# A softcap attention with a maxout layer behind it: another order of the same steps

## The chip, the cores and the metric

The kernel runs on one core of one Trainium2 chip. The metric is the device time of one execution in microseconds; three executions were timed, and a fourth was profiled. Engine names as in the profile: PE is TensorE, DVE is VectorE, ACT is ScalarE, POOL is GpSimd, SP is SyncE; PEld is TensorE's loading of weights.

## The reference

```python
batch, n_heads, seq, head_dim = (8, 12, 448, 64)
scale = 1.0 / np.sqrt(q.shape[-1])
scores = scale * np.matmul(q, k.transpose(0, 1, 3, 2))
scores = cap * np.tanh(scores / cap)
scores = scores - np.max(scores, axis=-1, keepdims=True)
attn = np.exp(scores)
attn = attn / (np.sum(attn, axis=-1, keepdims=True) + 1e-09)
attn_out = np.matmul(attn, v)
# x: 3584 tokens of 768, the heads side by side
h1 = x @ w1          # 768 x 1024
h2 = x @ w2
g = np.maximum(h1, h2)
out = g @ w_out      # 1024 x 768
```

All inputs and the output are float32 in memory; the cap is 30.

## The kernel before

**The mathematics it uses.** max(h1, h2) is h2 + relu(h1 - h2). So the kernel forms wd = w1 - w2 once (six chunks of 128 rows; `sub c e`, line 392, on DVE for e = 0 and on POOL for e = 1) and wm = w2 @ w_out once (the "premultiply": transposes of w2 `W`, copies `WC`, matmuls `P`, copies `PC`). Then out = relu(x @ wd) @ w_out + x @ wm. No maximum is subtracted before the exponential, since the tanh bounds the scores.

**Pairs and batches.** Two heads make a pair i (48 of them), two pairs make a double pair t (24), three of these a batch b. For pair i the scores are made in three key blocks j of 128 keys (`S i j`, line 502, into one of two score tiles in PSUM, s0 and s1), `T i j` is the tanh (line 507), `E i j0 j1` the exponential (line 524), both on ACT. The last 64 keys of both pairs of t are done together: `L t`, `TL t`, `EL t`. Exponentials are multiplied with v: `VL t` and `V t u j0 j1` (line 595), which also live in a score tile. `Y t` (line 561) sums the exponentials with a matmul by ones; from t = 3 on DVE has added the blocks before it (`A`, `B`, lines 536 and 541). Then DVE turns the sums to one column per 32 (`Y1`, line 566), takes the reciprocal (`Y2`, 569), turns it back (`Y3`, 572), and multiplies: `N t 0` (607, one instruction) and `N t 1` (610, two). The result is xT, the input of the dense part, in bfloat16. `N t 1` also frees the score tile that V t wrote, and `S 2t+3 2` is the next to use that tile.

**The dense part.** 120 groups g of matmuls: for each batch eight of stage 1 (relu(x @ wd), 448 columns, six units) and then three or four tiles times two halves of stage 2 (384 columns, fourteen units, 6 from x @ wm and 8 from g @ w_out). `O g bank` opens a group in one of four PSUM banks; `M x y n` (line 634) runs n steps, in each of which group x uses the upper 64 rows of TensorE and group y the lower 64 at the same time; -1 is none, x = y is one full step (line 629). A group's two halves add into one bank, one after the other: between them stands a hand-over, `Hs g` (a no-operation in SP's queue) or `H g` (in DVE's queue), which waits for the first half's last matmul and for which the second half waits. `ev g` copies a finished group out of PSUM on DVE: relu to gT (line 655, 448 columns) or to the output tile osb (line 691, 384 columns). `st b t` stores a tile from SP's queue. The dense steps fill TensorE's time between the steps of attention.

**The order.** It is written out as one string, ORDER: a list of steps. The kernel issues them one by one; each engine gets its instructions in that order, and a scheduler adds only the semaphores. So the string settles, for every engine by itself, what stands in front of what. Steps of different engines do not wait for each other unless data or a buffer make them.

**Loads.** All loads but the first k and q go through POOL's queue: `lk`, `lq`, `lv` (k, q, v of a pair or double pair), `lw1 c`, `lw2 c` (a chunk of w1 or w2), `lwo half part` (a part of w_out). They take eight semaphores in turn; a load waits until the load eight places before it has landed. From pair 10 on q and k are turned by a DMA transpose in SP's queue (`cr t`); before, by TensorE (`Xh`, `X`, copied by `XCh`, `XC`, line 453). `D bank n` are n matmuls on a constant tile, issued while TensorE has nothing else in the head.

The lines that run the string:

```python
    for s in ORDER.split(";"):
        if s.strip():
            name, *args = s.split()
            STEPS[name](*[int(a) if a.lstrip("-").isdigit() else a for a in args])
```

and those that tell which score tile a step takes:

```python
    TURN = (0, 1, 0, 1, 1, 0)
    def s_tile(turn, t):
        return s_psum.tile([P, 2, 512], f32, name=f"s{turn ^ (t % 2)}")
```

## Time and profile before

| what | value |
| --- | --- |
| three executions | 340.76, 341.51, 338.12 us; median 340.76 |
| the profiled execution | 337.93 us |
| its span, first to last instruction | 335.9 us, so 2.0 us lie around it |
| TensorE's granted clock | 0.998 |
| matmuls | 4,216 |
| bytes moved by the DMAs | 45.91 MB, mean 137 GB/s |
| largest group on ACT | L507 (tanh), 144 instructions, 925 ns each, 126.0 us |
| largest groups on PE | L634: 115.5, 101.4 and 96.4 us busy |
| L634 of wd (448 columns), one matmul | 349 ns; the two halves of a step run beside each other, and steps overlap |
| L655 copy with relu, DVE | 64 of 621 ns |
| L691 copy to osb, DVE | 54 of 555 ns |

How to read it: PE's records are pipelined, so that their durations overlap; from start to start a step of 448 columns takes 0.19 us, one of 384 columns 0.16. A wait is named with the engine that ended it ("PE s L502 <- DVE xT L610": scores on TensorE waited for DVE's writing of xT). POOL's instructions include the issuing of loads, about 0.5 to 0.9 us each.

The span has three stretches: a head up to about 57 us, in which weights are loaded and prepared and the first three double pairs are computed; a middle up to about 298 us, in which attention and dense steps are mixed; a tail of dense steps alone.

### The profile page before, as it was taken

Reading aid. Unit: us, or ns where it says so; the run is one execution under the profiler, and the core shown is the slowest. Engines: PE = TensorE matmul, PEld = TensorE weight load, DVE = VectorE, ACT = ScalarE, POOL = GpSimd, SP = SyncE. Lnnn points to the kernel's source line nnn. Section 1 sums busy time; section 2 is a strip of 40 time slices with the busy share of each in tenths; the row PEclk is TensorE's granted clock in tenths of the full one; section 3 lists DMA queues with packets and bytes.
Section 4 is the critical chain, followed back from the end, with each engine's and each line's share of the span. In section 5 each row is a group of like instructions: output and inputs, shape, how many; then the busy total and the mean of one; then the engine's idle time right before and its main releaser. Section 6 shows DMA issues by size and latency. Waiting matters only on the chain.

```text
span 335.9 us, 9947 instructions
## 1 busy us (share of the span) xinstructions
PE 322.6 (96%) x4216; PEld 196.7 (59%) x4216; DVE 244.2 (73%) x430; ACT 276.5 (82%) x267; POOL 175.4 (52%) x257
## 2 busy tenths in 40 slices
PE   8799999999999999999999999999999999999993
PEld 6654444566456555655555565675566555757972
DVE  1146879888788887987798789967988879785321
ACT  4699998999999999999999999989999999900000
POOL 7586879957645664853864687367188220000000
PEclk9999999999999999999999999999999999999999
DMA  8999999999999999989999999999999953013033
GB/s 131 203 160 229 152 251 109 158 128 89 210 172 97 102 209 213 101 110 157 141 162 109 143 191 212 101 115 166 168 130 115 202 118 79 2 47 96 2 96 94
DMA packets 136204, 45.91 MB, mean 137 GB/s; under 512 B 116448, under 2 KB 131168, under 8 KB 136160
## 3 DMA queue, kind: packets, MB, share of 16 engines
q0 software_dynamic: 96416, 25.08, 75.9%
q1 hardware_dynamic: 39440, 19.86, 27.7%
q8 instruction: 33, 0.54, 0.6%
q10 hardware_dynamic: 304, 0.33, 0.3%
q14 instruction: 11, 0.09, 0.1%
HBM read 47.45 MB, written 11.01 MB: 174 GB/s over the span
## 4 chain that ended last, share of the span: by engine, by line
PE 73%; DMA 11%; DVE 5%; ACT 4%; POOL 3%; issue 2%; POOLq 0%; DVEq 0%
PE mm L634 55%; PE s L502 7%; PE s L595 6%; DMA wo_sb<-in_moe_w_out_dram 4%; DMA gT<-in_moe_w_dram 2%; DMA kqs<-in_k_dram 2%; ACT e L524 2%; DMA xT<-in_moe_w_dram 2%; PE s L516 2%; DVE xT L610 1%; PE mm L561 1%; PE s L587 1%; ACT e L507 1%; POOL wd_sb L392 1%; PE mm L629 1%
## 5 line engine op out<-in xcount | busy, mean ns | idle before, releaser
L507 ACT ACTIVATE e<-s 128x896 bf16<-128x896 f32 x144 | 126.0, 925 | 12.7 <-PE s L502 12.5
L524 ACT ACTIVATE e<-e 128x2688 bf16<-128x2688 bf16 (+2 forms) x72 | 122.8, 1707 | 0.0
L634 PE MATMUL mm<-wo_sb,gT 64*128 64x384 bf16 x864 | 115.5, 323 | 0.0
L634 PE MATMUL mm<-wm_sb,xT 64*128 64x384 bf16 x648 | 101.4, 323 | 0.1
L634 PE MATMUL mm<-xT,wd_sb 64*128 64x448 bf16 x768 | 96.4, 349 | 0.9 <-DVE wd_sb L392 0.7
L339 POOL DMA_DIRECT2D kqs<-in_k_dram x76 | 54.4, 719 | 59.2 <-DMA qkT<-kqs 58.4
L634 PEld LDWEIGHTS <-gT 64*128 64x128 bf16 x864 | 61.8, 94 | 22.4 <-issue 1.1
L634 PEld LDWEIGHTS <-wd_sb 64*128 64x128 bf16 x768 | 50.8, 94 | 25.5 <-DVE wd_sb L392 1.1
L634 PEld LDWEIGHTS <-xT 64*128 64x128 bf16 x648 | 51.5, 94 | 16.8 <-issue 1.2
L502 PE MATMUL s<-qkT 64*128 64x448 bf16 x288 | 52.3, 355 | 2.7 <-DVE xT L610 2.3
L357 POOL DMA_DIRECT2D vp<-in_v_dram x48 | 30.5, 641 | 28.5 <-PE s L502 28.2
L655 DVE TENSOR_SCALAR gT<-mm 128x448 bf16<-128x448 f32 x64 | 39.2, 621 | 5.4 <-PE mm L634 4.0
L691 DVE COPY osb<-mm 128x384 f32<-128x384 f32 x54 | 29.1, 555 | 19.0 <-PE mm L634 18.2
L595 PE MATMUL s<-e,vp 128*32 128x448 bf16 x576 | 36.4, 354 | 0.0
L339 POOL DMA_DIRECT2D kqs<-in_q_dram x38 | 35.1, 925 | 1.7 <-DMA osb<-in_moe_w_dram 1.0
L536 DVE TENSOR_TENSOR esum<-e 128x896 bf16<-128x896 bf16 x42 | 26.4, 629 | 10.7 <-ACT e L524 10.4
L502 PEld LDWEIGHTS <-qkT 64*128 64x128 bf16 x288 | 17.8, 94 | 23.6 <-issue 15.7
L610 DVE TENSOR_TENSOR xT<-s,inv 64x448 bf16<-64x448 f32 x48 | 29.9, 622 | 0.7
L701 ACT COPY osb<-mm 128x192 f32<-128x192 f32 x1 | 0.3, 319 | 36.5 <-DMA out_dram<-osb 36.5
L536 DVE TENSOR_TENSOR esum<-esum,e 128x896 bf16<-128x896 bf16 x42 | 26.2, 623 | 5.1 <-ACT e L524 4.2
L357 POOL DMA_DIRECT2D vl<-in_v_dram x48 | 29.5, 625 | 0.0
L566 DVE STREAM_TRANSPOSE st<-mm 128x448 f32<-128x448 f32 x24 | 15.6, 650 | 15.8 <-PE mm L561 13.9
(57 smaller groups left out, 282.6 us busy)
## 6 DMA issues: line engine op xcount, KB each, us to landing
out_dram<-osb SPq DMA_DIRECT2D x54, 192.0 KB, 4.1
vp<-in_v_dram POOLq DMA_DIRECT2D x38, 160.0 KB, 4.0
kqs<-in_q_dram POOLq DMA_DIRECT2D x47, 112.0 KB, 4.8
kqs<-in_k_dram POOLq DMA_DIRECT2D x76, 56.0 KB, 3.4
wo_sb<-in_moe_w_out_dram POOLq DMA_DIRECT2D x4, 384.0 KB, 6.6
osb<-in_moe_w_dram POOLq DMA_DIRECT2D x2, 512.0 KB, 5.3
osb<-in_moe_w_dram POOLq DMA_DIRECT2D x4, 256.0 KB, 6.4
kqs<-in_k_dram POOLq DMA_DIRECT2D x9, 112.0 KB, 5.6
```

What stands on the lines that cost most here:

```text
L339: nc.gpsimd.dma_start(out=to, in_=x)
L357: nc.gpsimd.dma_start(out=to, in_=x)
L502: nc.tensor.matmul(s[:, h, :S], k_of(t, o, h, j), q_of(t, o, h))
L507: nc.scalar.activation(expo[i][:, 2 * j : 2 * j + 2, :], slots[i, j][:, :, :S], AF.Tanh, scale=scale / cap)
L524: nc.scalar.activation(e, e, AF.Exp, scale=float(cap))
L536: nc.vector.tensor_add(d, e[:, 0:2, :] if j == 1 else d, e[:, 2 * j : 2 * j + 2, :])
L566: nc.vector.transpose(st.rearrange("p b c -> p (b c)"), sums[t][:, :S])
L595: nc.tensor.matmul(vals[t][place(m, u), u, :S], w[:, m, :], expo[2 * t + o][:, 2 * j + h, :], start=False, stop=(j == NJ - 1))
L610: nc.vector.tensor_mul(x[r : r + 64], vals[t][r : r + 64, u, :S], sums[t, 3][64 - r : 128 - r])
L634: ins = nc.tensor.matmul(self.ps, w[r], x[r], start=first, stop=self.at == [self.n, self.n]).ins
L655: nc.vector.tensor_relu(gT[b // 2][:, f, cs], ps)
L691: nc.vector.tensor_copy(o[:, hs], ps)
```

## The change

ORDER is replaced by another order of almost the same steps. Counted by step: 101 matmuls `D` instead of 104; `M` steps 1,177 in both, `P` steps 96 in both; `H` 21 instead of 17 and `Hs` 107 instead of 110; the banks of many groups differ. Ten copies of stage 2 (groups 100 to 103 and 112 to 117) are now `eva`, which copies on ACT instead of DVE. `sub 4` is on DVE instead of POOL, so that only `sub 5` is left on POOL. `lwo 0 0`, the first part of w_out, is the first load in POOL's queue. A step name `lw1s` is added and not used. Nothing in the functions changes but the table of steps.

The start, the stretch with the subtractions, the turns at t = 5, 11 and 17, and the turn into the tail (the rest of the string is left out; it is changed nearly throughout):

```diff
-ld0 k; ld0 q; ms0; lk 1 0; dm; ms; D 3 3; lw2 2; D 3 5; id; D 3 5; lwo 0 0; D 3 7; lq 1 0; D 3 5; lw2 0; cd k;
...
-D 3 2; XC 1; D 3 1; E 0 0 3; D 3 10; lv 0 0; D 3 1; L 0; D 3 19; lv 0 1; W 3 2; TL 0; D 3 4; WC 3; D 3 7;
-S 1 0; lv 0 2; W 1 3; T 1 0; W 2 0; lv 0 3; WC 1; W 0 1; EL 0; lk 4 0; WC 2; S 1 1; S 1 2; T 1 1; lq 4 0; WC 0;
...
-V 1 1 2 3; Y1 1; sub 5 1; S 5 0; OP 3 1 0; P 3 1 2; Y2 1; P 3 1 2; Y3 1; P 2 1 3; T 5 0; P 2 1 1; N 1 0; O 0 2;
-M 0 -1 1; X 6 1; lw1 2; EL 2; N 1 1; lw1 1; S 5 1; T 5 1; PC 2 1; S 5 2; lq 8 0; XC 6; T 5 2; W 4 3; lw1 4;
-S 6 0; E 5 0 2; lk 8 0; WC 4; X 7 1; lk 9 0; S 6 1; XC 7; lq 9 0; OP 4 0 3; P 4 0 3; sub 2 0; T 6 0; P 4 0 1;
...
-E 6 0 3; lk 11 0; X 8 3; Y1 2; V 2 0 2 3; lk 11 1; XC 8; V 2 1 2 3; S 7 0; Y2 2; X 9 0; lv 3 0; T 7 0; Y3 2;
-lv 3 1; OP 5 1 3; P 5 1 2; XC 9; P 5 1 1; EL 3; P 5 1 1; sub 4 1; S 7 1; N 2 0; P 5 0 2; T 7 1; P 5 0 1; N 2 1;
-P 5 0 1; P 5 1 4; OP 4 1 0; P 4 1 3; PC 5 0; lv 3 2; S 7 2; S 8 0; PC 5 1; lv 3 3; T 7 2; P 4 1 2; A 3 0 1;
-P 4 1 2; lv 4 0; P 4 1 1; E 7 0 2; sub 3 0; M 0 -1 1; S 8 1; lv 4 1; M 0 -1 1; lv 4 2; PC 4 1; M 0 -1 2; T 8 0;
...
-V 5 1 2 3; Y1 5; S 13 0; M 13 12 1; lv 7 0; M 13 12 1; Y2 5; M 13 12 3; Y3 5; lv 7 1; O 14 3; M 14 12 2; Hs 13;
...
-V 11 1 2 3; Y1 11; S 25 0; lk 30 1; M 43 42 2; Y2 11; M 43 42 3; Y3 11; lv 13 0; M 43 42 3; T 25 0; st 2 1;
...
-V 23 0 2 3; V 23 1 2 3; Y1 23; M 100 101 1; ev 100; O 103 3; M 103 101 3; Y2 23; M 103 102 2; ev 101;
-M 103 102 3; Y3 23; M 103 102 4; N 23 0; M 103 102 2; O 104 1; M 104 102 2; N 23 1; Hs 103; M 104 102 1;
...
+ld0 k; ld0 q; ms0; lwo 0 0; dm; ms; D 3 5; lw2 2; D 3 5; lk 1 0; D 3 5; id; D 3 5; lq 1 0; D 3 3; cd k; D 3 1;
...
+XC 1; D 3 11; lwo 0 1; D 3 1; L 0; D 3 13; TL 0; D 3 6; lk 3 0; D 3 1; W 3 2; D 3 1; lq 4 0; D 3 1; S 1 0;
+WC 3; T 1 0; lv 0 0; W 1 3; EL 0; W 2 0; lv 0 1; WC 1; W 0 1; lv 0 2; WC 2; S 1 1; S 1 2; lv 0 3; T 1 1; WC 0;
...
+V 1 1 0 2; Y 1 0; lv 2 3; sub 0 0; E 4 0 3; V 1 0 2 3; V 1 1 2 3; Y1 1; S 5 0; O 0 1; M 0 -1 1; lq 7 0;
+P 3 0 2; Y2 1; P 2 1 1; Y3 1; lw1 2; P 2 1 2; T 5 0; X 6 0; lw1 1; N 1 0; P 2 1 1; EL 2; P 3 0 1; N 1 1; S 5 1;
+sub 5 1; P 3 0 2; T 5 1; P 3 0 1; XC 6; S 5 2; PC 2 1; T 5 2; W 4 0; PC 3 0; S 6 0; E 5 0 2; WC 4; OP 3 1 2;
+P 3 1 1; lk 8 0; X 7 3; lw1 4; S 6 1; XC 7; lq 8 0; P 3 1 2; T 6 0; P 3 1 1; sub 2 0; OP 4 0 0; P 4 0 1;
...
+P 4 0 1; E 5 2 3; L 3; PC 3 1; VL 2; V 2 0 0 2; TL 3; PC 4 0; V 2 1 0 2; lq 11 0; Y 2 3; sub 4 0; E 6 0 3;
+lk 10 0; V 2 0 2 3; X 8 2; Y1 2; lk 10 1; V 2 1 2 3; XC 8; S 7 0; lk 11 0; X 9 0; Y2 2; T 7 0; Y3 2; lk 11 1;
+M 0 -1 2; EL 3; N 2 0; OP 5 0 3; P 5 0 1; lv 3 0; S 7 1; P 5 0 1; N 2 1; P 5 0 1; T 7 1; P 5 0 1; OP 5 1 2;
...
+P 4 1 2; lv 4 2; P 4 1 1; sub 3 0; P 4 1 3; T 8 0; lv 4 3; P 4 1 1; A 3 1 1; lk 12 0; T 8 1; M 0 -1 1; S 8 2;
...
+V 5 0 0 2; V 5 1 0 2; Y 5 0; E 12 0 3; V 5 0 2 3; V 5 1 2 3; Y1 5; S 13 0; M 13 11 1; lv 7 0; M 13 11 1; Y2 5;
...
+V 11 0 2 3; V 11 1 2 3; Y1 11; S 25 0; lk 30 0; M 43 41 2; Y2 11; M 43 42 2; Y3 11; lv 13 0; M 43 42 4; N 11 0;
...
+M 100 101 4; Y 23 3; V 23 0 2 3; V 23 1 2 3; Y1 23; M 100 101 3; Y2 23; O 103 3; M 103 101 2; Y3 23; eva 100;
+M 103 101 1; M 103 102 2; eva 101; M 103 102 1; N 23 0; M 103 102 3; N 23 1; M 103 102 5; O 104 0; M 104 102 3;
...
```

Steps between Y t and S 2t+3 2 that stand on PE and DVE, counted in the whole strings:

| t | M steps before | on DVE between Y1 and N t 1, beside the chain | M steps after | on DVE after |
| --- | --- | --- | --- | --- |
| 5 | 10 | none | 18 | none |
| 11 | 15 | A 12 0 1 | 18 | none |
| 17 | 18 | ev 71, A 18 0 1 | 18 | none |
| 12 | 18 | ev 46 | 22 | ev 46, ev 47 |
| 15 | 20 | ev 60, H 62 | 18 | ev 61 |

## The prediction

> **What bounds the kernel now.** I read the page's engine shares first, then the chain that ended last, then who waited for whom, then the timeline around the longest waits.

> ```profile
> span 335.9 us, 9947 instructions
> PE 322.6 (96%) x4216; PEld 196.7 (59%) x4216; DVE 244.2 (73%) x430; ACT 276.5 (82%) x267; POOL 175.4 (52%) x257
> PE 73%; DMA 11%; DVE 5%; ACT 4%; POOL 3%; issue 2%; POOLq 0%; DVEq 0%
> PE s L502 <- DVE xT L610: 2.3, 4, 0.8
> ```

> TensorE is the bound: 96% busy, 73% of the chain. Its work cannot shrink here. Counted in both orders, the M steps number 1,177, with the same 1,131 pairs, 18 single halves and 28 full steps; at 384 or 448 columns per step they stream for 200.5 us in each. So the time can change only through TensorE's pauses: in the head, which ends at 57.28 us, in the middle, and at the turn into the tail. The last row above is the pause of the middle: scores that wait for VectorE's normalisation (N t 1) to free a score tile. The worst of them, t = 11, on VectorE, then TensorE, then ScalarE:

> ```profile
> 156.60 0.65 DVE L566 STREAM_TRANSPOSE st<-mm 128x448 f32<-128x448 f32 x1 [0.74 <-PE mm L561]
> 157.29 0.24 DVE L569 RECIPROCAL rs<-st 128x14 f32<-128x14 f32 x1
> 157.56 0.65 DVE L572 STREAM_TRANSPOSE inv<-rs 128x448 f32<-128x448 f32 x1
> 158.27 0.62 DVE L536 TENSOR_TENSOR esum<-e 128x896 bf16<-128x896 bf16 x1
> 158.82 0.62 DVE L607 TENSOR_TENSOR xT<-s,inv 128x448 bf16<-128x448 f32 x1
> 159.47 1.26 DVE L610 TENSOR_TENSOR xT<-s,inv 64x448 bf16<-64x448 f32 x2
> ```
> ```profile
> 159.63 0.35 PE L634 MATMUL mm<-xT,wd_sb 64*128 64x448 bf16 x1
> 160.78 0.55 PE L502 MATMUL s<-qkT 64*128 64x448 bf16 x4 [0.79 <-DVE xT L610]
> ```
> ```profile
> 159.78 0.92 ACT L507 ACTIVATE e<-s 128x896 bf16<-128x896 f32 x1
> 161.18 0.92 ACT L507 ACTIVATE e<-s 128x896 bf16<-128x896 f32 x1 [0.48 <-PE s L502]
> ```

> The five VectorE steps Y1, Y2, Y3, N t 0, N t 1 are a chain; S 25 2 starts 0.06 us after it. A pair of 448 columns takes 0.19 us from start to start, so 160.78 - 159.63 - 0.19 = 0.96 us are lost (0.79 in the modelled row). ScalarE loses 0.48. Two rows also show that dependent VectorE steps need no rest: 0.04 us from the end of Y1 to Y2, and 0.03 to Y3.

> The head is a chain through loads, GpSimd and VectorE. Its rows are of POOL's timeline, of the table by stretches (its last three columns are TensorE's clock, the DMA share and GB/s), of VectorE's and of TensorE's timeline:

> ```profile
> 36.70 2.69 POOL L392 TENSOR_TENSOR wd_sb<-xT,gT 128x1024 bf16<-128x1024 f32 x1
> 39.36 0.56 POOL L377 DMA_DIRECT2D osb<-in_moe_w_dram  x1
> ```
> ```profile
> 39.00:40.50 1.50, 1.50 (x31) 0.79 (x31) 1.38 (x3) 1.50 (x3) 1.50 (x4) 1.00 0.27 40
> ```
> ```profile
> 49.15 0.65 DVE L566 STREAM_TRANSPOSE st<-mm 128x448 f32<-128x448 f32 x1 [0.77 <-PE mm L558]
> 50.27 0.62 DVE L453 COPY qkT<-mm 128x896 bf16<-128x896 bf16 x1 [0.47 <-PE mm L448]
> 55.02 1.06 DVE L536 TENSOR_TENSOR esum<-e 128x896 bf16<-128x896 bf16 x1
> 56.01 1.21 DVE L392 TENSOR_TENSOR wd_sb<-osb,gT 128x1024 bf16<-128x1024 f32 x1
> ```
> ```profile
> 57.28 0.93 PE L634 MATMUL mm<-xT,wd_sb 64*128 64x448 bf16 x4 [0.69 <-DVE wd_sb L392]
> ```

> While GpSimd subtracts it issues no load, and the DMAs fall to 40 GB/s between 39.0 and 40.5 us. Later VectorE is packed from 49.15 to the end of sub 3 at 57.22, and TensorE waits for that.

> **The change, part by part.**

> *The middle, t = 3 to 22.* For each t I set the chain on VectorE, from Y1 to N t 1 with all that stands between, against TensorE's work between Y t and S 2t+3 2; 0.4 us are added to the chain for the way from the matmul Y to Y1 (156.18 to 156.60). The chain alone is 0.65 + 0.24 + 0.64 + 0.62 + 1.25 = 3.40. Before: t = 5 has 10 steps of cover, 2.48 us, so 1.32 are missing; t = 11 has 15 steps (3.28), and a sum of 0.63 stands in the chain: 1.15 missing; t = 17 has 18 steps (3.76), but a copy of 0.55 and a sum of 0.63 in the chain: 1.22 missing; t = 9, 12 and 18 miss 0.32; all others 0.19 or less. From start to start the trace has 1.27, 0.96 and 0.78 at t = 5, 11 and 17, 0.23 at t = 12 and 18, none at t = 9: 3.47 us. The count therefore finds the right places and is high by 0.1 to 0.4. After: t = 5, 11 and 17 all have 18 steps and nothing in the chain, 0.04 missing; t = 9, 15 and 21 miss 0.32, t = 3, 6, 12 and 18 0.19, the others 0.05 or less. By the rows of before the three cost 0 to 0.23 each and the rest nothing: 0 to 0.7, and I take 0.5. Gain 3.0 (2.7 to 3.5).

> *Banks and hand-overs.* The step that opens a bank waits for its old tile's copy. Before, groups 36, 51 and 81 miss 0.25 us by the same count; after, the tightest groups have 0.18 to spare. The loss before is under 0.13 us at each, so I book nothing. 21 hand-overs (H) now stand in VectorE's queue instead of 17, 107 instead of 110 in SyncE's. At the 17 no TensorE pause is seen, and at those of SyncE none over 5 ns: nothing, with a rival below.

> *Head, loads.* The first part of w_out goes to the front of POOL's queue, past w2 chunk 2 and k 1, and so k 1 lands later. Its user X 1 waits for q 1 in any case, landed at 10.73 behind the same five transfers: nothing, while q 1 stays behind k 1. All three are still ahead of the rest, so the w2 chunks land as before (14.2 us for the one that W 3 2 waits for). S 1 0 follows two warm-up matmuls instead of eleven, 9 x 0.053 = 0.48 us earlier; ScalarE, idle for 2.55 us there, starts that much earlier. q 4, k 6, k 7 and w2 chunk 4 are moved ahead of v and w1 loads. A k or q adds about 0.55 us to what lands behind it, chunk 4 up to 2.0; the loads put back had 2 us or more between landing and first use (v 0: 21.2 and 23.4; w1 chunk 0: 33.9 and 36.2; v 2: 36.8 and 47.1), and chunk 5's user, sub 5, moves back itself: nothing. sub 5 (GpSimd) now stands behind the issues of w1 chunks 2 and 1: these land up to 39.36 - 36.70 = 2.7 us earlier, and the last input of X 8 before 49.55. The 0.47 us that VectorE waited for X 8 go. Its cover is then VectorE's own chain.

> *Head, the subtraction.* sub 4 leaves GpSimd (2.14 us there) for VectorE, 1.22 us, directly ahead of Y1 2. It waits there for w1 chunk 4 (landed at 47.97), and behind it are Y1 2, the copy of X 8 and so N 2, which S 7 2 waits for. VectorE idled 0.77 there, so 0.45 are exposed; the 0.48 of ScalarE's earlier start can take them back. In the chain Y1 2 to sub 3, 8.07 us, a sum of 0.63 comes in (0.55 as it overlaps its neighbour), 0.47 of waiting go, and the 1.06 us of the sum that ran beside GpSimd's subtraction become 0.63: 7.7. Start 49.1, end 56.8 against 57.22. Lower end: ScalarE's start counts in full and VectorE waits for nothing, -1.0; upper end: chunk 4 lands where it did, 47.97, and 1.22 come on top unhidden, +1.2. I take -0.3.

> [...] The sum at 55.02 overlaps GpSimd's subtraction (53.45 to 55.59) for 0.57 us and takes 0.44 longer than its like. [...]

> *Tail.* ScalarE copies ten tiles (a 128x192 copy is 0.32 us, 128x896 0.92, so an estimate of 0.5 for 384 columns); it has been idle since 294.7. The two early ones free VectorE while N 23 is due. At 297.6 TensorE loses 0.28 for a bank; it now has three steps of cover more: -0.2 (0 to -0.3). The other eight wait for TensorE in ScalarE's queue, with nothing behind them but each other and the last store's half; the last store is unchanged.

> Sum: -3.0 - 0.3 - 0.2 = -3.5 on the profiled execution's 337.93 us, so 334.4 there. That execution is 2.83 under the median of the runs, 340.76, and the four known executions have their middle at 339.4. 340.76 - 3.5 = 337.3 and 339.4 - 3.5 = 335.9; I say 336.5.

> **Rivals.** (a) *ScalarE takes it back.* Its steps of one t, from start to start, sum to 11.26 us, and a t of the middle takes 11.4 to 12.2. At t = 5 it ran without a break while TensorE lost its 1.27. If only what ScalarE lost returns, 0.48 + 0.77 at t = 11 and 17, the gain is 1.25 + 0.5 = 1.8: 338.2. Against it: the end is TensorE's alone, 33 us after ScalarE's last exponential, so steps pulled forward shorten it. (b) *The head gives more:* -1.0 there and no residue in the middle: -4.7, 335.3. (c) *Slower: hand-overs in VectorE's queue.* In 10 of the 21 a copy of up to 0.62 us stands directly before the H (4 of 17 before), and TensorE's next step waits for both. At 0.17 us each the gain is gone (3.5 / 21); at 0.33 the kernel is 1% slower; at 0.42, 5.3 us of new loss, it gives 342.2. For it: H 8, 38 and 68 have two steps (0.37) after the copy. Against: H 32, 62 and 92 had a copy before them as well and cost nothing. (d) *No effect:* the new order has the old pauses under other names: 340.8. The waits' places are counted from the order itself, which speaks against it.

> **How the numbers follow.** About 1%, or 3.4 us, is what a measurement of this kernel tells from no change, given runs from 338.12 to 341.51. Chances: forecast 0.52, (a) 0.16, (b) 0.17, (c) 0.09, (d) 0.06. The forecast stands on the 1% border: I count 0.30 of its 0.52 as faster, with 0.16 of (b): 0.46. Slower by over 1%: 0.06 of (c). Same: 0.48. The range takes the sum's ends, -1.2 to -4.7, on middles of 338.1 to 341.5: 333.4 to 340.3.

> **What would show it.** Right: no wait of scores on xT over 0.3 us at t = 5, 11 and 17; VectorE's Y1, Y2, Y3, N rows unbroken there; w1 chunk 2 issued before GpSimd's subtraction, and no 40 GB/s stretch; sub 3 done by 57 us. Wrong: TensorE waiting for VectorE behind H, sub 4 late for its load, or ScalarE without any idle time while TensorE waits for it.

## The result, and the profile after

| kernel | median of runs | lowest to highest |
| --- | --- | --- |
| after, 20 runs | 336.37 us | 333.99 to 338.94 |
| before, 20 runs beside them | 338.44 us | 336.91 to 342.52 |

The ratio is 0.9928, with a 95% interval of 0.9900 to 0.9957: 2.4 us less (1.5 to 3.4); the medians differ by 2.07. The profiled execution of after took 337.60 us, 1.2 above its median; that of before, 337.93, was 0.5 below the median of these later runs. So the two traces must not be subtracted as a whole, but stretch by stretch.

The page of after, by span, engines and chain, and the row of waits that answers to "PE s L502 <- DVE xT L610" (each line number is one higher now):

```profile
span 335.6 us, 9954 instructions
PE 323.2 (96%) x4213; PEld 189.7 (57%) x4213; DVE 240.1 (72%) x421; ACT 281.2 (84%) x277; POOL 172.7 (51%) x256
PE 81%; DMA 10%; DVE 3%; POOL 3%; issue 1%; ACT 0%; POOLq 0%; ACTq 0%; DVEq 0%
```
```profile
PE s L503 <- DVE xT L611: 1.3, 2, 0.8
```

Two waits are left where there were four (the second figure of the row), and TensorE's part of the chain is up from 73% to 81%. Both waits are in the head; the middle has none that this view shows.

The turn at t = 11, in the timelines of VectorE, TensorE and ScalarE (start, duration, engine, line, and in brackets an idle time before the row and what ended it):

```profile
157.85 0.65 DVE L567 STREAM_TRANSPOSE st<-mm 128x448 f32<-128x448 f32 x1 [0.53 <-PE mm L562]
158.53 0.24 DVE L570 RECIPROCAL rs<-st 128x14 f32<-128x14 f32 x1
158.81 0.65 DVE L573 STREAM_TRANSPOSE inv<-rs 128x448 f32<-128x448 f32 x1
159.56 0.62 DVE L608 TENSOR_TENSOR xT<-s,inv 128x448 bf16<-128x448 f32 x1
160.22 1.26 DVE L611 TENSOR_TENSOR xT<-s,inv 64x448 bf16<-64x448 f32 x2
```
```profile
161.37 0.35 PE L635 MATMUL mm<-xT,wd_sb 64*128 64x448 bf16 x1
161.53 0.38 PE L503 MATMUL s<-qkT 64*128 64x448 bf16 x2
```
```profile
161.41 1.72 ACT L508 ACTIVATE e<-s 128x896 bf16<-128x896 f32 x2
```

The five VectorE steps stand next to each other, with no sum between. They end at 161.48, S 25 2 starts at 161.53, 0.16 after the pair before it, and ScalarE's two tanh run on without a break. From start to start, and from 62 us on, TensorE's pauses over 0.13 us at t = 5, 11, 12, 17, 18 and at the turn into the tail were 1.27, 0.96, 0.23, 0.78, 0.23 and 0.28 us; after, only three of 0.15 to 0.16 are left, at t = 9, 15 and 21.

The head did not become shorter. GpSimd's issues and subtraction 5, then VectorE's subtractions 1 and 4, Y1 2 and subtraction 3, then TensorE's and ScalarE's waits behind them:

```profile
39.42 0.55 POOL L378 DMA_DIRECT2D osb<-in_moe_w_dram  x1 [0.61 <-DMA xT<-in_moe_w_dram]
39.96 0.53 POOL L381 DMA_DIRECT2D osb<-in_moe_w_dram  x1
...
41.20 2.15 POOL L393 TENSOR_TENSOR wd_sb<-xT,gT 128x1024 bf16<-128x1024 f32 x1
```
```profile
48.93 1.22 DVE L393 TENSOR_TENSOR wd_sb<-osb,gT 128x1024 bf16<-128x1024 f32 x1 [1.61 <-DMA kqs<-in_q_dram]
...
51.01 1.21 DVE L393 TENSOR_TENSOR wd_sb<-xT,gT 128x1024 bf16<-128x1024 f32 x1
52.14 0.64 DVE L567 STREAM_TRANSPOSE st<-mm 128x448 f32<-128x448 f32 x1
...
58.81 1.22 DVE L393 TENSOR_TENSOR wd_sb<-osb,gT 128x1024 bf16<-128x1024 f32 x1
```
```profile
60.08 0.36 PE L635 MATMUL mm<-xT,wd_sb 64*128 64x448 bf16 x1 [0.58 <-DVE wd_sb L393]
```
```profile
56.57 0.92 ACT L508 ACTIVATE e<-s 128x896 bf16<-128x896 f32 x1 [1.77 <-PE s L503]
```

w1 chunk 2 is now issued ahead of GpSimd's subtraction, and yet at 39.42, where it was 39.36: its issue waits for the second half of chunk 5, the load eight places before, which landed at 39.13 (35.87 before). Chunk 1 landed at 48.85 instead of 46.57, and VectorE's subtractions 1 and 4 and Y1 2 follow it without a gap. Subtraction 3 ends at 60.03 in this execution.

### The profile page after: what moved, and what is told of

The parts are those of the page before. It is cut to its first block, busy times and chain, and to the rows that moved or that the text cites. A ratio compares the mean times of both kernels' runs of the same rounds, so it can differ in the third digit from the quotient of the medians.

```text
span 335.6 us, 9954 instructions
## 1 busy us (share of the span) xinstructions
PE 323.2 (96%) x4213; PEld 189.7 (57%) x4213; DVE 240.1 (72%) x421; ACT 281.2 (84%) x277; POOL 172.7 (51%) x256
## 4 chain that ended last, share of the span: by engine, by line
PE 81%; DMA 10%; DVE 3%; POOL 3%; issue 1%; ACT 0%; POOLq 0%; ACTq 0%; DVEq 0%
PE mm L635 59%; PE s L596 8%; PE s L503 8%; DMA kqs<-in_q_dram 3%; DMA gT<-in_moe_w_dram 3%; DMA vp<-in_v_dram 2%; DMA xT<-in_moe_w_dram 2%; PE s L517 2%; PE mm L562 2%; PE mm L630 1%; PE s L588 1%; DVE wd_sb L393 1%; POOL kqs L333 1%; DVE wm_sb L428 1%; POOL wo_sb L370 0%
## 5 line engine op out<-in xcount | busy, mean ns | idle before, releaser
L340 POOL DMA_DIRECT2D kqs<-in_k_dram x76 | 54.6, 721 | 56.8 <-DMA qkT<-kqs 56.0
L635 PEld LDWEIGHTS <-gT 64*128 64x128 bf16 x864 | 58.4, 94 | 25.6 <-issue 0.7
L635 PEld LDWEIGHTS <-wd_sb 64*128 64x128 bf16 x768 | 49.0, 94 | 26.7 <-issue 1.1
L635 PEld LDWEIGHTS <-xT 64*128 64x128 bf16 x648 | 50.6, 94 | 18.8
L596 PE MATMUL s<-e,vp 128*32 128x448 bf16 x576 | 36.8, 354 | 0.0
L503 PEld LDWEIGHTS <-qkT 64*128 64x128 bf16 x288 | 18.7, 94 | 22.1 <-issue 14.2
L690 ACT COPY osb<-mm 128x384 f32<-128x384 f32 x10 | 4.8, 478 | 26.9 <-PE mm L635 26.7
L692 DVE COPY osb<-mm 128x384 f32<-128x384 f32 x44 | 23.3, 553 | 5.1 <-PE mm L635 4.6
L542 DVE TENSOR_TENSOR esum<-esum,el 64x896 bf16<-64x896 bf16 x42 | 26.0, 619 | 1.2
```

What stands on the lines that cost most here:

```text
L340: nc.gpsimd.dma_start(out=to, in_=x)
L503: nc.tensor.matmul(s[:, h, :S], k_of(t, o, h, j), q_of(t, o, h))
L542: nc.vector.tensor_add(d, d, left_e[t][r, :, :])
L596: nc.tensor.matmul(vals[t][place(m, u), u, :S], w[:, m, :], expo[2 * t + o][:, 2 * j + h, :], start=False, stop=(j == NJ - 1))
L635: ins = nc.tensor.matmul(self.ps, w[r], x[r], start=first, stop=self.at == [self.n, self.n]).ins
L692: nc.vector.tensor_copy(o[:, hs], ps)
```

## The experiments

Each kernel was timed in 12 runs beside 35 of the kernel before (medians 338.56, 338.71 and 338.60 in the three sets). "Us" is the ratio less one, times 338.6, with its 95% interval.

| kernel | ratio, interval | us |
| --- | --- | --- |
| e1_first20 | 1.0023, 0.9997 to 1.0049 | +0.8 (-0.1 to +1.7) |
| e2_mid_head | 0.9987, 0.9958 to 1.0016 | -0.4 (-1.4 to +0.5) |
| e3_late | 0.9938, 0.9912 to 0.9964 | -2.1 (-3.0 to -1.2) |
| e4_old_start | 0.9941, 0.9908 to 0.9973 | -2.0 (-3.1 to -0.9) |
| e5_sub4_gpsimd | 0.9926, 0.9897 to 0.9955 | -2.5 (-3.5 to -1.5) |
| e6_sub4_vector | 1.0013, 0.9984 to 1.0042 | +0.4 (-0.5 to +1.4) |
| e7_t5_cover | 1.0008, 0.9982 to 1.0033 | +0.3 (-0.6 to +1.1) |
| e8_three_turns | 0.9990, 0.9960 to 1.0020 | -0.3 (-1.4 to +0.7) |
| e9_tail_only | 0.9993, 0.9962 to 1.0024 | -0.2 (-1.3 to +0.8) |
| e10_middle_only | 0.9958, 0.9930 to 0.9987 | -1.4 (-2.4 to -0.4) |
| e11_t5_cover_late | 1.0007, 0.9979 to 1.0036 | +0.2 (-0.7 to +1.2) |
| e12_sub5_later | 0.9973, 0.9943 to 1.0002 | -0.9 (-1.9 to +0.1) |

The intervals are wide against these differences. Two things make the reading sharper. The first is TensorE's clock. Each run's record has its mean granted clock; over the 268 runs of the changed kernel, of these twelve kernels and of the kernel before beside the twelve, the time goes with the clock that was lost (correlation 0.67, about 0.6 us for each us lost). In the fourteen traces the clock falls only up to 64 us and after the last matmul (in after from 11.12 to 14.53 us and from 335.38 on). So for the six kernels whose edits all stand behind that, a straight line in the clock lost, fitted to a kernel's runs and those of before beside them, takes that part of the scatter out. This is an estimate from the records, not a further run:

| kernel | us, with the clock taken out |
| --- | --- |
| e3_late | -2.0 (-2.5 to -1.5) |
| e7_t5_cover | +0.7 (+0.2 to +1.2) |
| e8_three_turns | -0.2 (-0.7 to +0.3) |
| e9_tail_only | -0.2 (-0.7 to +0.4) |
| e10_middle_only | -1.6 (-2.1 to -1.1) |
| e11_t5_cover_late | 0.0 (-0.4 to +0.5) |

The second is the traces. ScalarE's timeline marks the stretches: the start of TL 1, TL 4 and TL 7 and the end of the last exponential (E 47 2 3) cut each span in five (e6 is left out: its traced run, 342.85 us, in which TensorE stood 4.4 us for a late load, is the longest of its twelve and is in no ratio):

| kernel | to TL 1 | TL 1 to TL 4 | TL 4 to TL 7 | TL 7 to last exp | rest |
| --- | --- | --- | --- | --- | --- |
| before | 24.10 | 36.95 | 35.09 | 198.56 | 41.26 |
| after | 24.50 | 38.22 | 34.97 | 196.96 | 40.97 |
| e1 | 24.60 | 38.33 | 35.09 | 198.54 | 41.27 |
| e2 | 24.40 | 37.36 | 34.97 | 198.55 | 41.19 |
| e3 | 24.07 | 36.97 | 35.09 | 196.96 | 40.98 |
| e4 | 24.54 | 35.68 | 34.97 | 196.96 | 41.10 |
| e5 | 24.27 | 38.05 | 35.55 | 196.96 | 41.07 |
| e7 | 24.27 | 36.98 | 35.63 | 198.71 | 41.11 |
| e8 | 24.50 | 36.71 | 35.63 | 197.62 | 41.20 |
| e9 | 24.77 | 37.45 | 35.09 | 198.55 | 40.81 |
| e10 | 24.66 | 36.63 | 35.09 | 196.97 | 41.40 |
| e11 | 25.75 | 36.52 | 35.09 | 198.55 | 41.11 |
| e12 | 24.82 | 38.22 | 35.09 | 198.81 | 41.10 |

From TL 4 on, kernels with the same order agree within 0.3 us, but for e5 (35.55 beside 34.97), in whose trace the clock stood at half from 60.0 to 63.4 us. Up to TL 4 they do not: TL 1 to TL 4 runs from 36.52 to 38.33 in the seven experiments that keep the old order there. So most of a run's scatter is made in the head, and a single trace says little about it.

### First set: which stretch of the change does what

**e1_first20.** The changed order's first 89 steps, then the old order.

```diff
-ld0 k; ld0 q; ms0; lk 1 0; dm; ms; D 3 3; lw2 2; D 3 5; id; D 3 5; lwo 0 0; D 3 7; lq 1 0; D 3 5; lw2 0; cd k;
...
+ld0 k; ld0 q; ms0; lwo 0 0; dm; ms; D 3 5; lw2 2; D 3 5; lk 1 0; D 3 5; id; D 3 5; lq 1 0; D 3 3; cd k; D 3 1;
...
```

> The changed order up to about 20 us (w_out's first part at the front of POOL's queue, two warm-up matmuls ahead of S 1 0), the old order from there to the end. My theory: the head is where the change loses, and about half of it here: TensorE's silence before X 1 was 1.85 + 0.35 us instead of 1.62 in the changed kernel's trace, and its later loads v 0 landed at 24.11 instead of 20.78, which made VL 0 wait 0.82 instead of 0.35. So +0.4 to +1.0 us on the kernel before. Rival (the prediction on record): the moved loads cost nothing and S 1 0 comes earlier, so -0.3 to 0. Second rival: it is one profiled execution's noise, 0.

Measured +0.8, not told apart from nothing. The traces show no cost in the first 20 us: TL 1 starts at 24.50 and 24.60 with the changed start, and at a median of 24.50 in the eleven traces with the old one. The +0.8 has another place in this trace: TensorE waits 1.93 us, from start to start, for S 5 2, because VectorE's subtraction 0 took 3.03 us instead of 1.22. VectorE's and GpSimd's rows of e1:

```profile
36.69 3.03 DVE L383 TENSOR_TENSOR wd_sb<-osb,gT 128x1024 bf16<-128x1024 f32 x1
```
```profile
36.47 2.15 POOL L383 TENSOR_TENSOR wd_sb<-xT,gT 128x1024 bf16<-128x1024 f32 x1
```

GpSimd's subtraction 5 came first, at 36.47, and until it ended at 38.62 VectorE's got almost nowhere: 1.1 us later it was done, and alone it takes 1.22. The clock then stood at half from 43.08 to 46.49; what each of the two cost is not told apart. In the trace of before VectorE was first, at 36.19, and took its 1.22, and GpSimd, from 36.70, took 2.69. So in both traces the one that started second took longer, by a little less than the time for which the two overlapped: VectorE's 3.03 are 1.81 over its 1.22, for an overlap of 1.93, and GpSimd's 2.69 are 0.54 over its 2.15, for one of 0.71. In the old order the two stand side by side, so chance decides: in e11 GpSimd was first, at 36.88 for 37.84, and VectorE lost 1.07 there as well (2.29 us, for an overlap of 1.19), in the other old-order traces nothing. The changed order takes them apart.

**e2_mid_head.** Old order to about 20 us and from TL 7 on, the changed one between.

```diff
-V 1 1 2 3; Y1 1; sub 5 1; S 5 0; OP 3 1 0; P 3 1 2; Y2 1; P 3 1 2; Y3 1; P 2 1 3; T 5 0; P 2 1 1; N 1 0; O 0 2;
...
+V 1 1 0 2; Y 1 0; lv 2 3; sub 0 0; E 4 0 3; V 1 0 2 3; V 1 1 2 3; Y1 1; S 5 0; O 0 1; M 0 -1 1; lq 7 0;
...
```

> The old order up to about 20 us and from about 97 us on; the changed order between (subtraction 4 on VectorE, subtraction 5 behind the issues of w1 chunks 2 and 1, t = 5 with 18 steps of cover). My theory: the turn at t = 5 gives -1.27, and the rest of the head between 20 and 60 us takes back 0.5 to 1.0 (a new pause of 0.75 before S 3 2 in the changed trace, 0.92 before S 7 2): -0.3 to -0.8 us. The prediction on record: -1.27 - 0.3 = -1.6.

-0.4, inside my range; the -1.6 of the prediction is outside the interval. The pause at t = 5 is gone in its trace, but TL 4 to TL 7 takes 34.97 instead of 35.09: of the 1.27 us only 0.12 are gained there. I had taken the small total for a loss in the head that eats a real gain. The third set shows why there was hardly a gain to eat.

**e3_late.** The mirror: old order up to TL 7, changed order after it (banks renumbered at the seam).

```diff
-V 11 1 2 3; Y1 11; S 25 0; lk 30 1; M 43 42 2; Y2 11; M 43 42 3; Y3 11; lv 13 0; M 43 42 3; T 25 0; st 2 1;
...
+V 11 0 2 3; V 11 1 2 3; Y1 11; S 25 0; lk 30 0; M 43 41 2; Y2 11; M 43 42 2; Y3 11; lv 13 0; M 43 42 4; N 11 0;
...
```

> The old order up to TL 7 (about 97 us), the changed order from there to the end: the turns at t = 11 and 17, and the tail with the copies on ScalarE. My theory: from start to start TensorE's pauses over 0.13 us from there on were 0.96, 0.23, 0.78, 0.23 and 0.28 before, 2.48 in sum, and 0.46 after: -2.0 us. Rival (ScalarE takes it back): only what ScalarE lost at t = 11 and 17 returns, 1.25, less 0.46: -0.8. Rival (hand-overs): 0 or more.

-2.1, as the first theory had it: this stretch alone holds nearly the whole change. The hand-overs in VectorE's queue cost nothing that can be seen.

**e4_old_start.** Old order to about 20 us, the changed one from there.

```diff
-ld0 k; ld0 q; ms0; lwo 0 0; dm; ms; D 3 5; lw2 2; D 3 5; lk 1 0; D 3 5; id; D 3 5; lq 1 0; D 3 3; cd k; D 3 1;
...
+ld0 k; ld0 q; ms0; lk 1 0; dm; ms; D 3 3; lw2 2; D 3 5; id; D 3 5; lwo 0 0; D 3 7; lq 1 0; D 3 5; lw2 0; cd k;
...
```

> The old order up to about 20 us, the changed order for all the rest: it undoes the first 20 us of the change alone. My theory: what the first 20 us cost returns, 0.4 to 1.0 us, so -2.5 to -3.4 us on the kernel before, and VL 0 waits 0.4 us or less. Rival: the first 20 us cost nothing, and it is as fast as the changed kernel, -2.1.

-2.0: no faster than the changed kernel, though VL 0 waits 0.35 as in before. With e1's TL 1 this speaks against my theory: these runs show no cost of the first 20 us. e1's interval, up to +1.7, does not rule one out.

### Second set: subtraction 4, and the turns by themselves

**e5_sub4_gpsimd** and **e6_sub4_vector**, each one step moved, in e4's kernel and in the kernel before:

```diff
-Y 2 3; sub 4 0; E 6 0 3;
+Y 2 3; E 6 0 3;
...
-lv 3 1; P 5 1 3;
+lv 3 1; sub 4 1; P 5 1 3;
```

> The kernel of e4_old_start with one step changed: subtraction 4 is back on GpSimd, two loads behind N 2 0. My theory: in the changed order VectorE is packed from subtraction 1 on, so the 1.22 us of subtraction 4 ahead of Y1 2 push N 2 1, S 7 2 and T 7 2 back, and ScalarE, which paces the stretch up to TL 7, waits for T 7 2 (0.84 us in e4's trace, 1.77 in the changed kernel's). Without it 0.5 to 1.0 us less than e4_old_start: -2.6 to -3.1 on the kernel before. The prediction on record has the move to VectorE as part of a gain of 0.3, so that undoing it costs: -1.8.

```diff
-Y 2 0; lk 10 1; E 6 0 3;
+Y 2 0; sub 4 0; lk 10 1; E 6 0 3;
...
-sub 4 1; S 7 1;
+S 7 1;
```

> The kernel before with one step changed: subtraction 4 on VectorE, ahead of Y1 2. My theory: 1.22 us less the 0.47 and 0.3 that VectorE idles there, of which the sum beside GpSimd's subtraction gives back 0.44: +0.1 to +0.9. The prediction on record: 0.45 exposed and taken back by other parts, so 0 to +0.45.

e5 is -2.5, half a microsecond below e4, with intervals that reach over each other by far; e6 is +0.4 (-0.5 to +1.4). Both lean to a cost of about 0.4 on VectorE, and neither shows it. e5's trace does not help: there a sum of VectorE beside GpSimd's subtraction 4 took 1.98 us instead of 0.62, and the clock fell as said. This stays open.

**e7_t5_cover** and **e8_three_turns.** e7:

```diff
-N 5 1; M 14 13 1; EL 6; S 13 1; lk 18 0; T 13 1; A 6 0 1; lk 18 1; S 13 2; M 14 13 1; M 12 13 2; Hs 14; T 13 2; A 6 0 2; M 12 13 1; lq 18 0; S 14 0;
+N 5 1; M 14 13 1; M 14 13 1; M 12 13 2; Hs 14; M 12 13 1; EL 6; S 13 1; lk 18 0; T 13 1; A 6 0 1; lk 18 1; S 13 2; T 13 2; A 6 0 2; lq 18 0; S 14 0;
```

> The kernel before with four M steps moved ahead of S 13 1 (cover at t = 5 of 14 steps instead of 10), nothing else. New theory: ScalarE paces t = 4 to 6 without a break, so TL 7 comes when it came, and the pause that goes returns as other waits of TensorE: 0 (+-0.2). The prediction on record, in which TensorE alone sets the end: 4 x 0.19 = 0.76 less.

+0.3: the -0.76 is outside the interval, if not by much, and far outside with the clock taken out (+0.2 to +1.2). But the edit had a fault of its own: S 13 1 stood behind the four steps, and ScalarE waited 0.44 for it, so that TL 4 to TL 7 took 35.63. e11 mends this. e8 is e7 with two more turns:

```diff
-M 43 42 3; T 25 0; st 2 1; A 12 0 1; M 43 42 1;
+M 43 42 3; T 25 0; st 2 1; M 43 42 1;
...
-A 12 0 2; S 25 2; S 26 0; lk 31 0; M 44 43 1;
+A 12 0 1; A 12 0 2; M 44 43 1; S 25 2; S 26 0; lk 31 0;
...
-M 73 72 3; A 18 0 1; lv 19 2;
+M 73 72 3; lv 19 2;
...
-A 18 0 2; st 4 1; S 37 2; S 38 0; M 74 73 1; T 37 2; lk 43 1; M 72 73 2;
+A 18 0 1; A 18 0 2; st 4 1; M 74 73 1; M 72 73 1; S 37 2; S 38 0; T 37 2; lk 43 1; M 72 73 1;
```

> The kernel before with the three turns cleared and nothing else: e7's four steps at t = 5, A 12 0 1 behind N 11 1 and one step more of cover at t = 11, A 18 0 1 behind N 17 1 and two steps more at t = 17. If TensorE alone sets the end: 0.76 + 0.82 + 0.78 = 2.4 us less. If ScalarE paces these stretches, only what ScalarE lost returns: 0 + 0.48 + 0.77 = 1.25 less at most.

-0.3 (-1.4 to +0.7): the 2.4 of TensorE alone are far outside. By the table t = 5 cost 0.54 here, as in e7, and TL 7 to the last exponential is 0.94 shorter. The pause at t = 11 fell from 0.96 to 0.28, and 0.26 came back at S 26 0. The sum of the two, -0.40, agrees with the -0.2 (-0.7 to +0.3) that is left with the clock taken out. Clearing a pause is not the same as gaining it.

### Third set: the parts by themselves

**e9_tail_only** (changed order from group 102 on) and **e10_middle_only** (changed order from TL 7 to group 101):

```diff
-V 23 0 2 3; V 23 1 2 3; Y1 23; M 100 101 1; ev 100; O 103 3; M 103 101 3; Y2 23; M 103 102 2; ev 101;
...
+M 100 101 4; Y 23 3; V 23 0 2 3; V 23 1 2 3; Y1 23; M 100 101 3; Y2 23; O 103 3; M 103 101 2; Y3 23; eva 100;
...
```

> The kernel before up to group 101 (about 293 us), the changed tail from there: ten copies on ScalarE. In e3's trace this stretch took 36.93 us where it took 37.34 before, and the pause of 0.28 us for a bank is gone: -0.3 to -0.4 us. The prediction on record: -0.2. Rival: the middle's gain was really the tail's, -1 or more.

```diff
-N 11 1; M 44 43 1; lv 13 3; T 25 1; lq 30 0; A 12 0 2; S 25 2;
+N 11 1; M 43 42 1; lv 13 2; M 43 42 1; O 44 3; M 44 42 2; EL 12; Hs 43; S 25 1;
...
```

> The old order up to TL 7 and from group 102 on, the changed order between (about 97 to 293 us, the turns at t = 11 and 17). In e3's trace that stretch was 1.39 us shorter. ScalarE's own waits at t = 11 and 17 (0.48 + 0.77 = 1.25) and TensorE's pauses (2.2 less 0.46 of residue = 1.74) both stand near it: -1.25 by the one, -1.74 by the other.

-0.2 and -1.4. In the traces TL 7 to the last exponential is 1.59 shorter in e10. The rest after it is 0.45 shorter in e9, but by the means of the table the changed tail takes 40.99 (five traces) and the old one 41.20 (eight): 0.2. Together they give 1.8, for e3's -2.1 (-3.0 to -1.2).

**e11_t5_cover_late.** The same four steps as in e7, behind S 13 1.

```diff
-T 13 1; A 6 0 1; lk 18 1; S 13 2; M 14 13 1; M 12 13 2; Hs 14; T 13 2; A 6 0 2; M 12 13 1; lq 18 0; S 14 0;
+T 13 1; A 6 0 1; lk 18 1; M 14 13 1; M 12 13 2; Hs 14; M 12 13 1; S 13 2; T 13 2; A 6 0 2; lq 18 0; S 14 0;
```

> As e7_t5_cover, but the four steps M stand between S 13 1 and S 13 2, so that S 13 1, which ScalarE waited 0.44 us for in e7, is not moved. If ScalarE paces t = 4 to 6: no wait of ScalarE at T 13 1, TL 6 to TL 7 in 11.41 us as before, time 0 (+-0.2). If TensorE sets the end: -0.76.

+0.2, TL 4 to TL 7 35.09, TL 6 to TL 7 11.41, as before. Of the three pauses that make the 1.27 (0.36 before a step M that waits for N 5 0, 0.30 before S 13 1, 0.61 before S 13 2) the edit clears the last, so TensorE alone would give -0.6. The plain interval reaches that far (-0.7); with the clock taken out (-0.4 to +0.5) it does not. The trace shows why. ScalarE and TensorE in the kernel before, at t = 5:

```profile
87.88 0.91 ACT L507 ACTIVATE e<-s 128x896 bf16<-128x896 f32 x1
88.68 0.95 ACT L527 ACTIVATE el<-el 128x896 bf16<-128x896 bf16 x1
89.52 1.72 ACT L507 ACTIVATE e<-s 128x896 bf16<-128x896 f32 x2
91.11 1.72 ACT L524 ACTIVATE e<-e 128x1792 bf16<-128x1792 bf16 x1
```
```profile
88.84 0.37 PE L502 MATMUL s<-qkT 64*128 64x448 bf16 x2
89.64 0.37 PE L502 MATMUL s<-qkT 64*128 64x448 bf16 x2 [0.43 <-DVE xT L610]
```

and in e11 (scores are line 493, tanh line 498 there):

```profile
89.11 0.91 ACT L498 ACTIVATE e<-s 128x896 bf16<-128x896 f32 x1
89.90 0.95 ACT L518 ACTIVATE el<-el 128x896 bf16<-128x896 bf16 x1
90.74 1.73 ACT L498 ACTIVATE e<-s 128x896 bf16<-128x896 f32 x2
92.34 1.71 ACT L515 ACTIVATE e<-e 128x1792 bf16<-128x1792 bf16 x1
```
```profile
90.92 0.36 PE L493 MATMUL s<-qkT 64*128 64x448 bf16 x2
91.71 0.36 PE L493 MATMUL s<-qkT 64*128 64x448 bf16 x2 [0.43 <-ACT e L498]
```

ScalarE's rows start at the same distances to 0.01 us, without a gap in either. The wait of S 13 2 for VectorE is gone, and the next scores, S 14 0, wait instead, 0.60 from start to start, for the tanh that frees their tile. The sum of the pauses is 1.27 in both.

**e12_sub5_later.**

```diff
-V 1 1 2 3; Y1 1; sub 5 1; S 5 0;
+V 1 1 2 3; Y1 1; S 5 0;
...
-lw1 2; EL 2; N 1 1; lw1 1; S 5 1;
+lw1 2; EL 2; N 1 1; lw1 1; sub 5 1; S 5 1;
```

> The kernel before with subtraction 5 (GpSimd) behind the issues of w1 chunks 2 and 1, nothing else. The prediction on record: the two chunks land up to 2.7 us earlier and VectorE's wait of 0.47 for X 8 goes: -0.3 or more. My theory: they are issued at 37.4 instead of 39.4, since the load eight places before has landed by then, but the DMAs set when they land: under 1 us earlier; 0 to -0.4 us.

-0.9 (-1.9 to +0.1), more than my theory had. The trace does not show the gain in the way that the prediction told: chunk 2 was issued at 38.09, but it landed at 46.79 and chunk 1 at 48.99, later than before, so the early issue was no early landing. What is gone is the meeting with subtraction 0. Whether that makes the 0.9, or whether it is scatter of the head, these runs do not settle.

None of the kernels is shown to be faster than the changed one. e3 with e12's move (-2.1 and -0.9) was not run.

## Why the prediction came out as it did

The time came out as forecast, 336.37 for 336.5, but by luck: two errors cancelled in it. The change is 2.1 to 2.4 us, not 3.5; and the middle from which I subtracted, 339.4 to 340.76, was high: the later runs of the kernel before have medians of 338.44 to 338.71.

- **Bound.** "TensorE is the bound", read from 96% against ScalarE's 82% of the span. But ScalarE is done at 294.7 us. The table by stretches of before, from TL 7 to the last exponential (columns: from:to, length, busy time of PE, PEld, DVE, ACT, POOL, then clock, DMA share, GB/s):

```profile
96.14:294.70 198.56, 197.02 (x2590) 118.06 (x2582) 162.84 (x287) 191.61 (x184) 104.70 (x148) 1.00 1.14 138
```

  ScalarE is busy for 191.61 of 198.56 us there, 96.5%. TensorE is busy for 197.02. Two engines are nearly full, and a pause of one counts only where the other has room: at t = 5 ScalarE had none, and in e11 TL 4 to TL 7 stayed at 35.09.

- **Middle, -3.0: the failed step.** It counted TensorE's 1.27 us at t = 5 in full. The prediction had the fact in hand, in rival (a): "At t = 5 it ran without a break while TensorE lost its 1.27", and set it aside with "Against it: the end is TensorE's alone" (and 33 us after ScalarE's last exponential; the last matmul ends 36.0 after it). It also put the whole 1.27 down to VectorE's chain, while 0.30 of it, before S 13 1, ends with a tanh: S 13 1 starts at 88.84, and the tanh that began at 87.88 is done at 88.79. e11 cleared the wait of S 13 2, 0.6 us, and gained nothing. The other two pauses were cleared only in the changed order, where 144 steps M instead of 138 stand between TL 4 and TL 7, and that stretch is 0.12 shorter. The six stood ahead of TL 4 in the old order, in the head; that TL 4 comes earlier for it does not show in these traces. Its own sign of being wrong, "ScalarE without any idle time while TensorE waits for it", is what e11's rows show.

  The spacing from one TL to the next tells it beforehand, in the trace of before. Around t = 5, 11 and 17 it is 11.41, 11.98 and 12.28 us (TL 6 to TL 7, TL 12 to TL 13, TL 18 to TL 19). ScalarE's own steps sum to 11.26; TensorE's own work, the spacing less its pauses, is 10.14, 11.02 and 11.50. What lies above the larger of the two is 0.15, 0.72 and 0.78 us, 1.65 in all, and the traces gain 0.12 and 1.59, 1.71. The prediction had 3.0.
- **The rest of the middle** was right: 0.96 + 0.78 + 0.46 less 0.5 is 1.7, for -1.4 (-2.4 to -0.4) in e10 and 1.59 to 1.60 in the traces. The residue of 0.5 stands where the count put it, at t = 9, 15 and 21, with 0.46. Rival (a)'s 1.25 lies in e10's interval too, also with the clock taken out (1.1 to 2.1); the times do not part them.
- **Hand-overs** in VectorE's queue: no pause over 0.13 us at any of them from 62 us on; rival (c) falls. Its last price was wrong besides: 21 times 0.42 is 8.8 us, which on the forecast gives 345.3, not 342.2.
- **Head, -0.3.** Its sum is not contradicted, its steps are. The warm-up matmuls, priced at 0.053 us each, start 0.056 apart in the trace of before. "these land up to 39.36 - 36.70 = 2.7 us earlier" failed, since the issue waits for the load eight places before it, and that one had moved back. The chain from Y1 2 to subtraction 3 was right in length, 7.7 for 7.89 here, 7.89 and 8.11 in e2 and e4, but it started at 52.14, 51.18 and 49.42 instead of 49.1, and ended 60.03, 59.07 and 57.53. TL 1 to TL 4 has a mean of 37.07 in the eight old-order traces up to e11 and of 37.09 in after, e2 and e4: no gain and no loss that shows in a scatter of 2 us. The parts that are shown, 1.6 and 0.2, leave 0.3 to 0.6 of the 2.1 to 2.4 us unplaced, within the noise.
- **Tail, -0.2:** -0.2 in e9, with a wide interval, and 0.2 by the means of the traces. ScalarE's copies took 478 ns, estimated at 0.5.

Of the rivals, (a) came nearest in size: 1.8 for 2.1 to 2.4. Its mechanism holds at t = 5, where e11 shows it; at t = 11 and 17 it is not told apart from TensorE's own pauses.

## What to carry to other kernels

Before a pause of the busiest engine is booked as a gain, set the length of that stretch against the sum of every other engine's work in the same stretch: what lies above the larger of the sums can go (here 1.65 us by this count, 1.71 in the traces), the rest comes back as another wait (in e11 as the 0.60 before S 14 0). Shares of the whole span hide this when an engine is done early: ScalarE's was 82% of the span, and 96.5% of the stretch from TL 7 to 294.7 us. And where a head full of loads makes the scatter, compare traces by stretches that repeat, times only over many runs, and look at whether the scatter goes with something that each run records.

## What the runs showed of the hardware

```profile
8.95:12.36 3.41, 1.74 (x45) 1.38 (x42) 0.62 (x1) 2.59 (x2) 1.61 (x3) 1.00 1.14 205
12.36:15.77 3.41, 3.41 (x38) 3.02 (x37) 0.00 (x0) 0.92 (x1) 2.83 (x5) 0.50 1.17 187
```
```profile
8.79:12.20 3.41, 1.86 (x51) 1.45 (x50) 0.62 (x1) 3.00 (x2) 1.12 (x3) 1.00 1.18 212
12.20:15.61 3.41, 2.36 (x46) 2.14 (x38) 0.43 (x1) 0.92 (x1) 2.07 (x4) 1.00 1.18 192
```

In the fourteen traces, from the first switch on, every stretch in which TensorE was busy for less than 1.86 us was followed by one at half clock, and every one with more kept full clock; at 1.86 both occur, and one stretch with 1.52 at the end of e6's tail kept it. In after the stretch ahead of the fall, from 7.70 to 11.12, was busy for 1.63, and one with 1.95, from 328.56 to 331.97, kept full clock; in before none up to the last matmul has less than 2.50. In e3 the silence of 2.13 us lay across the border of two stretches, the fuller share of it in one that was still busy for 1.92. What sets the 3.41 us is not shown here. TL 0 started at 12.39 to 12.81 without the fall and at 12.92 to 14.60 with it, TL 1 at 24.07 to 24.27 and 24.27 to 25.75. More matmuls D in that silence were not tried.

**A load issued earlier did not land earlier.** In this program a load's issue waits for the load eight places before: in after, w1 chunk 2 was issued at 39.42, behind the landing of chunk 5's second half at 39.13. And chunk 2 of w1 took 4.8 us from issue to landing in before, issued at 39.36, and 8.7 in e12, issued at 38.09. In before it met DMAs with little to do, 50 to 54 GB/s from 39 to 41 us; in e12 they moved 123 to 196 GB/s from 38 to 41.
